# Squares on TensorE, sums on GpSimd, a gather from unscaled rows and a new order of issue in a fused convolution and selection kernel

## The chip, the cores and the metric

The kernel runs on one core of a Trainium2 chip. The metric is the time of one execution on the device in microseconds (us), the median of several; a profile of one execution goes with each kernel. A run counts as slow when it is over 1.5% above the fastest run of the same kernel.

The names of engines in the profile's lines are PE (TensorE's matrix products), PEld (its weight loads), DVE (VectorE), ACT (ScalarE), POOL (GpSimd) and SP (the engine that issues most DMAs). PSUM holds the tiles that TensorE's products are written to (`ps`, `pq`, `pg` in the lines), and an evacuation is the operation that copies or multiplies them out of it.

## The reference, cut to what matters

```python
h = layernorm(A_q) * (1 + ca) + sa                      # 2048 tokens x 640
x = A_q + ga * (h * (long_conv(short_conv(A_k) * A_v, ssm_k) + ...))   # two FFTs, product, inverse FFT
h = layernorm(x) * (1 + cb) + sb
r = h @ w_r;  idx = the 8 tokens with the largest r
y = (silu(h[idx] @ w_gate) * (h[idx] @ w_up)) @ w_down * sigmoid(r[idx])
out = x + gb * (h, with y added at the 8 rows)
```

So there is a long front that makes the convolution, block by block of 128 columns (five blocks), with Fourier products on TensorE; a middle in which the last sums x are formed and the second layernorm's sums and sums of squares are taken; and an end: root, choice of the eight rows, their gather and projections, the blend of all rows, and a scatter-add of eight rows into the output.

## The kernel before: the parts that matter

All steps are generators, and one string gives the order in which their pieces are issued. A star after a name means "on VectorE" for pieces that can go to either engine.

```python
# ORDER, its last lines (letters: BT inverse product, AT last products and sums, R row products,
# P complex product, S/SV/SA squares, BS/BL base, T choice to scatter, N normalised rows, F blend,
# LU load of U, WG/WD weights; new in the change: AA the adds of AT, GR a square step on TensorE)
#  ... BT4:2 P4:2 R0 AT2:2
#  BT4:2 LU3 AT3 R1 AT3 R1 R2* BS*:2 R2 R3* LU4 AT4:2 BS* S:3 R3 R4* SV R4 S SA:2 WD BS:3 T BS:2 BL N:5 N* T N*
#  WG N* N:2 T N N* N:3 N* F T F:3 BL F T:2 F:3 T:4

psum = tile_pool(bufs=4)                       # four double PSUM buffers for everything
T2 = ring.tile([P, 8, 2, P], BF, tag="T2")     # ONE buffer

def t_P(b):                                    # complex product, for each half of a block
    V.tensor_tensor(out=T2, in0=X, in1=Hi, op=mult)
    V.tensor_tensor(out=X,  in0=X, in1=Hr, op=mult)
    V.tensor_tensor(out=Xr, in0=Xr, in1=T2[:, :, 1, :], op=subtract)
    V.tensor_tensor(out=Xi, in0=Xi, in1=T2[:, :, 0, :], op=add)

def t_AT(b):                                   # [cut: 16 products into ps]
    V.tensor_tensor(out=t, in0=ps, in1=h[...], op=mult)
    V.tensor_tensor(out=xq[:, :, cc], in0=xq[:, :, cc], in1=t, op=add)

def squares(b0, nb, ms):                       # ScalarE; 9 rows of one block by VectorE statistics
    for m in ms:
        nc.scalar.activation(out=junk, in_=xq[:, m, ...], func=Square, accum_out=dst[:, m:m+1])

def t_T():                                     # [cut]
    rsqrt(rs2, vv)                             # seed and three Newton steps
    # [cut: r_bf, choice of 8, onehot]
    matmul(pxs[:, b, :], lhsT=xn(m)[:, b*P:(b+1)*P], rhs=onehot[:, m, :])   # gather of NORMALISED rows
```

Of the kernel before, what the change touches and what calls it, by code (L numbers as in the profile page):

```python
# [9 lines left out]
P = 128  # L10
# [25 lines left out]
LK0 START TC RA DIAG0 RA TAB0 RAT LG0 LK1 C0:2 TAB0 G0 LG1 TAB1:2 G0*:2 LX G0* DIAG1 C1:2 DIAG2 BG0 LXA0 BG0*  # L36
IT* Sx RAT G1 BG0 G1:3 DIAG3 Sx:2 IT*:2 X0 X0* BG1 LXA1 X0 X0* BG1 LX:2 LW BG1:2 LK2 Sx:4 X1 BX0 BX0*:2 BX0
P0:2 X1:3 BG0 LG2 LW LK3 C2:2 MOD Sx DIAG4 Sx LX LW Sx:2 P0:2 G2:3 BT0 BX1 LXA2 C3 G2 BX1 BT0 Sx:2 BT0 BX1 MOD
LW MOD LW P1 BX1 X2:3 Sx:4 LG3 C3 X2 BT0 MOD LW LXA3 P1:2 LK4 BG2:2 BX2 LG4 P1 BX2:3 BG2:2 MOD:2 OG BT1 P2:4
G3 X3:2 BT1 COL G3:2 H:3 G3 G4:2 C4 BT1 H BT1 H X3:2 C4 LXA4 LU0 G4:2 BG3 BX3:2 H:3 BT2 H:4 BX3 BG3:3 BT2:3 P3  # L40
AT0 P3 LU1 X4:4 AT0 BX3 BG4 P3:2 BX4:3 BG4 AT1 WG BT3 LU2 BT3:3 BG4:2 P4:2 AT1 BX4 R0 BT4:2 P4:2 R0 AT2:2
BT4:2 LU3 AT3 R1 AT3 R1 R2* BS*:2 R2 R3* LU4 AT4:2 BS* S:3 R3 R4* SV R4 S SA:2 WD BS:3 T BS:2 BL N:5 N* T N*
WG N* N:2 T N N* N:3 N* F T F:3 BL F T:2 F:3 T:4
# [17 lines left out]
def _kernel_body(ctx, tc, A_q, A_k, A_v, A_shift_k, A_ssm_k, A_ssm_D,  # L61
# [5 lines left out]

    def dump(name, ap):
        if name in DBG:
            nc.sync.dma_start(out=DBG[name], in_=ap)  # L70
# [6 lines left out]
    psum = ctx.enter_context(tc.tile_pool(name="psum", bufs=4, space=bass.MemoryType.PSUM))  # L77

    def ps_tile(shape, dtype=F32):
        return psum.tile(list(shape), dtype, name="ps", tag="ps")  # L80
# [69 lines left out]
    bcol = const.tile([NB * NSEL, 1], F32, name="bcol")  # L150
    gb40 = const.tile([NB * NSEL, P], BF, name="gb40")
# [41 lines left out]
    def t_TC():  # L193
# [9 lines left out]
        G.tensor_scalar(out=bcol[:], in0=bcol[:], scalar1=-MAGIC, scalar2=None, op0=ALU.add)  # L203
        G.tensor_scalar(out=cinfo[:, 0:1], in0=mC[:], scalar1=128.0, scalar2=None, op0=ALU.mult)
# [60 lines left out]
    As, HXs, Uds, uAs, diags = {}, {}, {}, {}, {}  # L265
# [21 lines left out]
    def t_C(b):  # L287
        kT, vT = kTs[b], vTs[b]
        kvT = ring.tile([P, S_TOK], BF, name="kvT", tag="V")
        for i2 in range(2):  # L290
            ps = ps_tile([P, 2, 512])
            for i in range(2):
                n0 = 16 + 512 * (2 * i2 + i)
                for j in range(4):
                    nc.tensor.matmul(ps[:, i, :], lhsT=diags[b][:, j, :], rhs=kT[:, n0 - j:n0 - j + 512],  # L295
                                     start=(j == 0), stop=(j == 3))
            V.tensor_tensor(out=kvT[:, 1024 * i2:1024 * i2 + 1024], in0=ps[:].rearrange("p a b -> p (a b)"),  # L297
                            in1=vT[:, 1024 * i2:1024 * i2 + 1024], op=ALU.mult)
# [24 lines left out]
    T2 = ring.tile([P, 8, 2, P], BF, name="T2", tag="T2")  # L323

    def t_P(b):
        hx = HXs[b]
        for hk in range(2):
            ks = slice(8 * hk, 8 * hk + 8)
            X = hx[:, ks, :, 1, :]
            Xr, Xi = hx[:, ks, 0, 1, :], hx[:, ks, 1, 1, :]  # L330
            Hr, Hi = (hx[:, ks, i:i + 1, 0, :].to_broadcast([P, 8, 2, P]) for i in range(2))
            V.tensor_tensor(out=T2[:], in0=X, in1=Hi, op=ALU.mult)
            V.tensor_tensor(out=X, in0=X, in1=Hr, op=ALU.mult)  # L333
            yield
            V.tensor_tensor(out=Xr, in0=Xr, in1=T2[:, :, 1, :], op=ALU.subtract)
            V.tensor_tensor(out=Xi, in0=Xi, in1=T2[:, :, 0, :], op=ALU.add)
            yield

    def t_BT(b):
        hx = HXs[b]  # L340
        Ud = Uds[b] = dram.tile([P, M, 256], BF, name="Ud%d" % b)
        for hk in range(2):
            U = ring.tile([P, 8, 256], BF, name="U", tag="K", bufs=5)
            for kk in range(2):
# [8 lines left out]
                if kk == 1:  # L353
                    nc.gpsimd.dma_start(out=Ud[:, 8 * hk:8 * hk + 8, :], in_=U[:])  # L354
# [15 lines left out]
    ssq = small.tile([P, 2, M], F32, name="ssq")  # L370
# [4 lines left out]
    def t_AT(b):  # L375
        h = h_["h"]
        c0 = b * P
        for hb in range(2):
            uA = uAs[b][hb]
            ps = ps_tile([P, 2, M, 32])  # L380
            for bb in range(8):
                o = ps[:, bb // 4, :, (bb % 4) * 8:(bb % 4) * 8 + 8]
                for cs in range(2):
# [3 lines left out]
            t = ring.tile([P, M, 64], BF, name="t", tag="K", bufs=5)  # L387
            cc = slice(c0 + hb * 64, c0 + hb * 64 + 64)
            V.tensor_tensor(out=t[:].rearrange("p m (g j) -> p m g j", g=2), in0=ps[:].rearrange("p g m j -> p m g j"),  # L389
                            in1=h[:, :, cc].rearrange("p m (g j) -> p m g j", g=2), op=ALU.mult)  # L390
            V.tensor_tensor(out=xq[:, :, cc], in0=xq[:, :, cc], in1=t[:], op=ALU.add)  # L391
            yield

    def junk():
        if "junk" not in h_:
            h_["junk"] = ring.tile([P, S_TOK], BF, name="junk", tag="V")
        return h_["junk"]

    def squares(b0, nb, ms):

        dst = ssq[:, 0 if b0 == 0 else 1, :]
        n = nb * P
        for m in ms:
            nc.scalar.activation(out=junk()[:, 0:n], in_=xq[:, m, b0 * P:b0 * P + n], func=ACT.Square,  # L404
                                 accum_out=dst[:, m:m + 1])

    def t_S():
        for q in range(4):
            squares(0, 4, range(4 * q, 4 * q + 4))
            yield  # L410

    def t_SV():
        st = small.tile([P, 9, 2, 3], F32, name="st4")
        sq = small.tile([P, 9, 2], F32, name="sq4")
        for i in range(9):
            V.bn_stats(out=st[:, i].rearrange("p e s -> p (e s)"), in_=xq[:, 7 + i, 512:640])
        V.tensor_tensor(out=sq[:], in0=st[:, :, :, 1], in1=st[:, :, :, 1], op=ALU.mult)
        V.scalar_tensor_tensor(out=sq[:], in0=sq[:], scalar=64.0, in1=st[:, :, :, 2], op0=ALU.mult, op1=ALU.add)
        V.tensor_tensor(out=ssq[:, 1, 7:16], in0=sq[:, :, 0], in1=sq[:, :, 1], op=ALU.add)
        yield  # L420

    def t_SA():
        for ms in (range(0, 3), range(3, 7)):
            squares(4, 1, ms)
            yield
# [25 lines left out]
    def t_R(b):  # L451
# [3 lines left out]
        xT = ring.tile([P, M, P], BF, name="xT", tag="K", bufs=5)  # L455
        evac(xT[:], pt[:])
        yield
        pr = ps_tile([P, M, 3])
        for m in range(M):
            nc.tensor.matmul(pr[:, m, :], lhsT=xT[:, m, :], rhs=wcol[:, b, :], start=True, stop=True)  # L460
# [40 lines left out]
    def t_COL():  # L501
# [22 lines left out]
        onesf = early[:, 9728:9984].bitcast(F32)  # L524
        nc.gpsimd.memset(onesf, 1.0)
        pr = ps_tile([P, 2, 512])
        nc.tensor.matmul(pr[:, 0, 0:2], lhsT=onesf, rhs=red[:], start=True, stop=True)
# [26 lines left out]
    def rsqrt(dst, vv, name):  # L554
# [5 lines left out]
        V.tensor_scalar(out=vv[:], in0=vv[:], scalar1=-0.5, scalar2=None, op0=ALU.mult)  # L560
        y = yi[:].bitcast(F32)
        a = small.tile([P, n], F32, name=name + "a")
        for it in range(3):
            V.tensor_tensor(out=a[:], in0=y, in1=y, op=ALU.mult)
            V.tensor_tensor(out=a[:], in0=a[:], in1=vv[:], op=ALU.mult)
            o = dst if it == 2 else y
            V.scalar_tensor_tensor(out=o, in0=a[:], scalar=1.5, in1=y, op0=ALU.add, op1=ALU.mult)
# [10 lines left out]
    def t_S1():  # L578
# [5 lines left out]
        rsqrt(rs1[:], var1, "n1")  # L584
# [3 lines left out]
    def t_H():  # L588
        h = h_["h"] = big.tile([P, M, D], BF, name="h", tag="h")
        for m4 in range(4):  # L590
# [7 lines left out]
            V.tensor_tensor(out=hq, in0=hq, in1=sg[:, None, :].to_broadcast([P, 4, D]), op=ALU.add)  # L598
# [20 lines left out]
    rs2, nm2 = tiny("rs2"), tiny("nm2")  # L619
# [17 lines left out]
    def t_F():  # L637

        for j in range(8):
            x2 = xq[:, 2 * j:2 * j + 2, :]  # L640
            V.tensor_tensor(out=x2, in0=xn(2 * j, 2).rearrange("p (m d) -> p m d", m=2),  # L641
                            in1=gbo[:, None, :].to_broadcast([P, 2, D]), op=ALU.mult)
            V.tensor_tensor(out=x2, in0=x2, in1=h_["base", j // 4][:, 2 * (j % 4):2 * (j % 4) + 2, :], op=ALU.add)  # L643
            if j % 2 == 1:
                nc.sync.dma_start(out=out_d[:, 2 * j - 2:2 * j + 2, :], in_=xq[:, 2 * j - 2:2 * j + 2, :])
# [207 lines left out]
```

## Time and profile before

| | us |
|---|---|
| time, median of 3 runs (lowest, highest) | 186.27 (185.97, 188.59) |
| span of the profiled run | 183.9 |
| last inverse product (BT4) leaves TensorE: the front | 131.40 |
| from there to the start of `tot`, the variance: the middle | 22.03 |
| from `tot` to the end of `r_bf`: the root | 3.16 |
| from there to the end of the last blend F: the end | 18.59 |
| from there to the end of the span: the finish | 8.72 |

The five rows add up to the span. One more row, from a table by stretches of time, is wanted for comparison (columns: stretch, its length, busy time and number of instructions of PE, PEld, DVE, ACT, POOL, then granted clock, share of the DMA engines, GB/s):

```profile
0.00:131.40 131.40, 113.84 (x1134) 90.64 (x1134) 116.77 (x188) 103.20 (x112) 28.50 (x72) 0.97 0.92 234
```

VectorE works 116.77 of the front's 131.40 us and idles for 14.6.

### The profile page before, as it was taken

Reading aid. Unit: us, or ns where it says so; the run is one execution under the profiler, and the core shown is the slowest. Engines: PE = TensorE matmul, PEld = TensorE weight load, DVE = VectorE, ACT = ScalarE, POOL = GpSimd, SP = SyncE. Lnnn points to the kernel's source line nnn. Section 1 sums busy time; section 2 is a strip of 40 time slices with the busy share of each in tenths; the row PEclk is TensorE's granted clock in tenths of the full one; section 3 lists DMA queues with packets and bytes.
Section 4 is the critical chain, followed back from the end, with each engine's and each line's share of the span. In section 5 each row is a group of like instructions: output and inputs, shape, how many; then the busy total and the mean of one; then the engine's idle time right before and its main releaser. Section 6 shows DMA issues by size and latency. Waiting matters only on the chain.

```text
span 183.9 us, 4109 instructions
## 1 busy us (share of the span) xinstructions
PE 144.0 (78%) x1664; PEld 112.5 (61%) x1664; DVE 157.7 (86%) x283; ACT 136.2 (74%) x180; POOL 33.2 (18%) x81
## 2 busy tenths in 40 slices
PE   0669989985989999939999969999679578165850
PEld 0225979952768679837679759998577342024840
DVE  5869998988979899977599999989979996999930
ACT  4368789792897979775599979999448999996000
POOL 7997500005001022010010020020200102100003
PEclk9999999999999999995799999999999999955555
DMA  6999989999999999992041999994768099705540
GB/s 108 152 204 278 313 186 326 272 198 274 265 292 320 338 304 309 176 200 114 0 171 61 212 320 324 368 338 183 200 261 224 8 293 362 310 4 219 207 153 2
DMA packets 68668, 40.68 MB, mean 221 GB/s; under 512 B 44904, under 2 KB 64808, under 8 KB 68648
## 3 DMA queue, kind: packets, MB, share of 16 engines
q1 hardware_dynamic: 65160, 35.15, 72.7%
q0 software_dynamic: 1520, 5.25, 7.7%
q10 hardware_dynamic: 1968, 0.01, 0.7%
q8 instruction: 13, 0.21, 0.5%
q14 instruction: 7, 0.06, 0.1%
HBM read 24.67 MB, written 10.50 MB: 191 GB/s over the span
## 4 chain that ended last, share of the span: by engine, by line
DVE 27%; DMA 27%; PE 24%; ACT 12%; issue 6%; SPq 2%; POOLq 1%; POOL 0%; DVEq 0%; ACTq 0%
DMA kT<-in_A_k_dram 9%; PE ps L295 8%; ACT junk L404 7%; DMA kvd<-kvT 7%; DMA uA<-Ud 6%; DVE kvT L297 4%; DVE st L581 4%; PE ps L274 3%; PE ps L314 3%; DVE xq L641 3%; DMA Ud<-U 3%; DVE xq L643 3%; PE ps L384 2%; ACT U L58 2%; ACT A L58 2%
## 5 line engine op out<-in xcount | busy, mean ns | idle before, releaser
L58 ACT CAST A<-ps 128x1024 bf16<-128x1024 f32 x35 | 33.6, 1030 | 8.5 <-PE ps L274 8.5
L58 ACT CAST HX<-ps 128x1024 bf16<-128x1024 f32 x37 | 35.9, 1054 | 2.8 <-PE ps L318 2.8
L314 PE MATMUL ps<-A,FT 128*128 128x256 bf16 x160 | 36.2, 272 | 0.4 <-DVE kvT L297 0.4
L318 PE MATMUL ps<-A,FT 128*128 128x128 bf16 x160 | 35.0, 219 | 0.0
L316 PE MATMUL ps<-A,FT 128*128 128x128 bf16 x160 | 35.0, 219 | 0.0
L295 PE MATMUL ps<-kT,dg 128*128 128x512 bf16 x80 | 21.6, 426 | 7.0 <-DMA kT<-in_A_k_dram 7.0
L58 ACT CAST U<-ps 128x1024 bf16<-128x1024 f32 x20 | 19.8, 1048 | 5.0 <-PE ps L350 2.3
L295 PEld LDWEIGHTS <-dg 128*128 128x128 bf16 x80 | 8.5, 108 | 17.4 <-issue 3.8
L354 POOL DMA_DIRECT2D Ud<-U x10 | 5.7, 572 | 72.9 <-ACT U L58 62.9
L348 PE MATMUL ps<-IT,HX 128*128 128x256 bf16 x80 | 18.1, 273 | 0.8 <-DVE kvT L297 0.8
L350 PE MATMUL ps<-IT,HX 128*128 128x256 bf16 x80 | 18.1, 273 | 0.0
L297 DVE TENSOR_TENSOR kvT<-ps,vT 128x1024 bf16<-128x1024 f32 x10 | 12.1, 1220 | 6.9 <-PE ps L295 5.7
L318 PEld LDWEIGHTS <-FT 128*128 128x128 bf16 x160 | 15.7, 98 | 1.8
L316 PEld LDWEIGHTS <-FT 128*128 128x128 bf16 x160 | 15.6, 98 | 0.9 <-issue 0.8
L314 PEld LDWEIGHTS <-FT 128*128 128x128 bf16 x160 | 15.7, 98 | 0.3
L237 POOL TENSOR_SCALAR dg<-ident,shk_f 128x128 bf16<-128x128 bf16 x16 | 10.3, 659 | 20.0 <-PE ps L295 20.0
L384 PE MATMUL ps<-RAT,uA 128*128 128x128 bf16 x160 | 10.4, 219 | 4.2 <-DMA uA<-Ud 4.2
L404 ACT ACTIVATE junk<-xq 128x512 bf16<-128x512 bf16 (+1 forms) x23 | 12.2, 533 | 2.0 <-DVE xq L391 1.3
L389 DVE TENSOR_TENSOR t<-ps,h 128x1024 bf16<-128x1024 f32 x10 | 12.2, 1218 | 1.7 <-PE ps L384 1.6
L581 DVE BATCH_NORM_STATS2 st<-xq 128x6 f32<-128x320 bf16 x32 | 13.2, 478 | 0.5 <-DMA xq<-in_A_q_dram 0.5
L274 PE MATMUL ps<-RA,gA 128*128 128x256 bf16 x80 | 12.3, 309 | 1.5 <-DVE gA L281 1.5
L333 DVE TENSOR_TENSOR HX<-HX 128x2048 bf16<-128x2048 bf16 x10 | 12.2, 1225 | 0.4
(218 smaller groups left out, 308.6 us busy)
## 6 DMA issues: line engine op xcount, KB each, us to landing
Ud<-U POOLq DMA_DIRECT2D x10, 512.0 KB, 6.0
uA<-Ud SPq DMA_DIRECT2D x10, 512.0 KB, 6.5
early<-in_w_mod_dram SPq DMA_DIRECT2D x6, 800.0 KB, 7.3
gA<-in_A_ssm_k_dram SPq DMA_DIRECT2D x5, 512.0 KB, 5.0
kvd<-kvT SPq DMA_DIRECT2D x10, 256.0 KB, 3.9
xq<-in_A_q_dram SPq DMA_DIRECT2D x4, 640.0 KB, 6.4
xA<-kvd SPq DMA_DIRECT2D x5, 512.0 KB, 4.8
out_dram<-xq SPq DMA_DIRECT2D x4, 640.0 KB, 3.1
```

The lines of the kernel that those rows point to most:

```text
L58: self.nc.scalar.copy(out=out, in_=in_)
L274: nc.tensor.matmul(ps[:, bb // 2, :, (bb % 2) * 8:(bb % 2) * 8 + 8], lhsT=src[:, 4 * g4 + bb, :], rhs=RA[:].rearrange("p k c e -> p (k c) ...
L295: nc.tensor.matmul(ps[:, i, :], lhsT=diags[b][:, j, :], rhs=kT[:, n0 - j:n0 - j + 512], start=(j == 0), stop=(j == 3))
L297: V.tensor_tensor(out=kvT[:, 1024 * i2:1024 * i2 + 1024], in0=ps[:].rearrange("p a b -> p (a b)"), in1=vT[:, 1024 * i2:1024 * i2 + 1024], ...
L314: nc.tensor.matmul(ps[:, i], lhsT=FT[:, 0, k2, :], rhs=A[:, 2 * k2:2 * k2 + 2, u, :], start=True, stop=False)
L316: nc.tensor.matmul(ps[:, i, 0, :], lhsT=FT[:, 1, k2, :], rhs=A[:, 2 * k2 + 1, u, :], start=False, stop=False)
L318: nc.tensor.matmul(ps[:, i, 1, :], lhsT=FT[:, 2, k2, :], rhs=A[:, 2 * k2, u, :], start=False, stop=True)
L348: nc.tensor.matmul(ps[:, i, :], lhsT=hx[:, k2, 0, 1, :], rhs=IT[:, k2, 1:3, :].rearrange("p a b -> p (a b)"), start=True, stop=False)
L350: nc.tensor.matmul(ps[:, i, :], lhsT=hx[:, k2, 1, 1, :], rhs=IT[:, k2, 0:2, :].rearrange("p a b -> p (a b)"), start=False, stop=True)
L384: nc.tensor.matmul(o, lhsT=uA[:, bb, cs * P:(cs + 1) * P], rhs=RAT[:, cs, :].rearrange("p (m e) -> p m e", e=8), start=(cs == 0), stop=(cs ...
L404: nc.scalar.activation(out=junk()[:, 0:n], in_=xq[:, m, b0 * P:b0 * P + n], func=ACT.Square, accum_out=dst[:, m:m + 1])
L581: V.bn_stats(out=st1[:, m, hf, :], in_=xq[:, m, hf * 320:hf * 320 + 320])
```

## The change

The intent: take the squares from ScalarE (TensorE forms small products of the transposed rows, whose diagonals are the sums of squares), take sums from VectorE (starred ones go to GpSimd), make the gather independent of the normalised rows, shorten the root, and reorder everything.

```diff
-LK0 START TC RA DIAG0 RA TAB0 ...                  (the whole order is new)
+LK0 START RA LG0 DIAG0 ... LG3 TC P1* ...          (TC, small constants on GpSimd, comes late)
+... BT4* BT4 AT1 AA1* AT1 R0* LU3 AA1 AT2*:2 AA2* LU4
+R0 R1 WG AT3 GR AA2 R1 AT3 AA3* R2 AT4 GR AT4 AA3* AA4* R2 R3* BS AA4 GR R3 R4* GR BS GR WD GR R4 BS:4 T:2 N*
+BS:2 N*:2 T BL F N:5 BL N:3 T N F T:2 N:4 F:6 T:4
+def off(): return nc.gpsimd if evac.vector else V
+def times(out, acc, other):          # starred: ScalarE copies acc first, VectorE multiplies; else as before
-psum bufs=4
+psum: three double buffers "ps", one single bank "pq" for small products, one single bank "pg"
-V.tensor_tensor(out=Xr, ...); V.tensor_tensor(out=Xi, ...)          (t_P; the adds of t_AT and t_H alike)
+off().tensor_tensor(out=Xr, ...); off().tensor_tensor(out=Xi, ...)
-nc.gpsimd.dma_start(out=Ud...)
+(nc.sync if b == NB - 1 else nc.gpsimd).dma_start(out=Ud...)
-squares(...) on ScalarE, bn_stats on VectorE
+def t_GR():                          # one step for each block, 64 products; squares' sums stay in PSUM
+    for m in range(16):
+        for j in range(4):
+            matmul(pg[32j:32j+32, m, :], lhsT=xT[:, m, 32j:32j+32], rhs=xT[:, m, 32j:32j+32], tile_position=(0, 32j))
+    after the last: V multiply by a diagonal mask, V reduce -> ssq
-rsqrt: three Newton steps
+rsqrt: two steps of higher order, constant folded into the users
-matmul(pxs, lhsT=xn(m) ...)                         gather of normalised rows
+matmul(pxs, lhsT=xq[:, m, ...] ...)                 gather of unscaled rows; their scales and shifts are
+sel = onehot * (rs2, nm2); reduce; matmul(ones, sel2); five small ops give xsT
-store of four row groups after every second F    ->  +store of two after every F
```

## The prediction

> **What bounds the kernel now.** I read the page first (busy shares, slices), then a table by stretches of time, then the chain that ended last, then each engine's timeline from 128 us on.
>
> ```profile
> span 183.9 us, 4109 instructions
> PE 144.0 (78%) x1664; PEld 112.5 (61%) x1664; DVE 157.7 (86%) x283; ACT 136.2 (74%) x180; POOL 33.2 (18%) x81
> ...
> 100.00:120.00 20.00, 18.02 (x224) 16.45 (x222) 19.69 (x23) 18.20 (x20) 1.43 (x3) 1.00 0.98 290
> ...
> 140.00:150.00 10.00, 6.53 (x119) 5.33 (x117) 9.93 (x15) 9.59 (x27) 0.63 (x1) 1.00 0.55 149
> 150.00:160.00 10.00, 5.93 (x29) 2.36 (x26) 7.97 (x42) 9.78 (x24) 1.51 (x5) 1.00 1.02 375
> 160.00:170.00 10.00, 5.29 (x86) 3.44 (x86) 9.69 (x19) 8.66 (x11) 0.52 (x2) 0.55 0.27 98
> ```
>
> The columns of the table are PE, PEld, DVE, ACT, POOL busy, then granted clock, DMA share, GB/s. VectorE (DVE) is the fullest engine in the front and again after 160 us; GpSimd (POOL) is nearly empty; TensorE's clock falls to 0.55 at the end.
>
> Three stages follow. Front, to about 131.4 us, where the last inverse-transform products (BT4) leave TensorE: from the windows, VectorE is busy 115.4 of the first 130 us. Middle, to 153.4, where the variance can start. End, the root, the choice of 8 rows, the normalised rows N, the blend F and the last scatter. The ends of the last two:
>
> ```profile
> 143.42 1.07 PE L384 MATMUL ps<-RAT,uA 128*128 128x128 bf16 x16 [0.71 <-DMA uA<-Ud]
> ...
> 138.33 0.63 ACT L404 ACTIVATE junk<-xq 128x512 bf16<-128x512 bf16 x1 [1.31 <-DVE xq L391]
> ...
> 153.43 0.17 DVE L653 SCALAR_TENSOR_TENSOR tot<-ssq 128x16 f32<-128x16 f32 x1 [1.09 <-ACT junk L404]
> ...
> 167.82 0.22 PE L715 MATMUL ps<-onehot,IT 128*128 128x8 bf16 x2 [0.62 <-ACT IT L633]
> ...
> 174.36 0.82 DVE L643 TENSOR_TENSOR xq<-xq,base 128x1280 bf16<-128x1280 bf16 x1
> 175.10 0.26 DVE L740 TENSOR_TENSOR hT<-gs,ps 128x112 bf16<-128x112 bf16 x1
> ```
>
> The last block of sums waits for a DMA round trip (U written, uA read): U ready 132.6, second half used at 143.4. The squares fill ScalarE for 15 us, 138.3 to 153.3, and VectorE's variance waits 1.09 us for them: their removal alone is worth about that, because the row products for the last block reach VectorE only at 151.7. The gather waits repeatedly for rows normalised by ScalarE. But the last blend op ends at 175.2 and hT comes right after it, while the second projection was done at 174.4: gather and blend are nearly tied, so speeding the gather alone gains under 1 us.
>
> **What the Trainium skill says.** (1) "SBUF — State Buffer", Who interferes with whom: VectorE and GpSimd share a port pair under an exclusive lock; a VectorE op with two SBUF inputs shuts out a GpSimd op that reads SBUF, and the reverse. The trace agrees: a 16-column GpSimd add, usually 0.27 us, took 1.24 us, ending just after the VectorE product that began before it:
>
> ```profile
> 68.57 1.22 DVE L333 TENSOR_TENSOR HX<-HX 128x2048 bf16<-128x2048 bf16 x1
> ...
> 68.68 1.24 POOL L281 TENSOR_TENSOR gA<-gA,Dt 128x16 bf16<-128x16 bf16 x1 [2.16 <-DMA gA<-in_A_ssm_k_dram]
> ```
>
> (2) "GPSIMD Engine Reference", Elementwise — side-by-side cycle accounting: about 2.6 cycles an element for two inputs at 1.2 GHz. My estimate for 1024 columns is 1024 x 2.6 / 1.2 = 2.2 us, against 0.69 on VectorE here; no large GpSimd add is in this trace. (3) "TensorE: Matmul & The Clock Gate", Wait — 56ns, not 53.3ns?: starts of small matmuls are never closer than about 25 ns. Here 70 projection products take 2.0 us, 28.6 ns each, agreeing roughly. (4) "TensorEngine Tiling (Array Packing)", Restrictions: column tiling disables fast weight load. No product here is tiled, so its cost is open.
>
> **The change part by part.** I counted the schedule's steps with start-to-start times from the timelines: a PSUM evacuation 1.13 us on VectorE, 0.91 on ScalarE; a complex-product half 2.4 (two products) plus 1.22 (two sums); a block half of AT 1.13 plus 0.61 for the add.
>
> Front. Evacuations put on VectorE before the end of BT4 rise from 11 (3 G, 1 BG, 3 IT, 2 X, 2 BX) to 20 (6 G, 1 BG, 3 IT, 6 X, 3 BX, 1 BT): +10.2 us. Six pairs of sums of the complex product go to GpSimd: -7.3. AT steps before the end of BT4 fall from six to two, and one add is done by then: 10.4 down to 2.9, so -7.5. Small differences (one convolution evacuated by ScalarE, two shorter roots) take about 1. Summed over the two orders, the large work is 112.8 us before BT4 ends now and 107.0 after: -5.8. The front now loses 131.4 - 112.8 = 18.6 us to idling and small ops; with the same loss BT4 would end at 125.6. The better order can trim it, lock and PSUM can add.
>
> Middle. AT and its add for four blocks are moved here, and the squares. Each new square step is 64 products of 32x32 (four column tiles for each of 16 row groups); at 28 ns, 1.8 us, five of them 9 us. From the end of BT4, TensorE has eight AT steps of 0.9 (7.2), five transposes of 0.9 (4.5), five row products of 0.44 (2.2), 9.0 for squares and two base steps of 0.87 (1.7): 24.6 us. Then multiply and reduce over 512 columns, about 0.65 each[...], and the last row sum 0.2: 1.5. The variance can start at +26.1, against 153.4 - 131.4 = 22.0 now. TensorE, not ScalarE, would set this stage: +4.1. ScalarE's 15 us are freed, but were only just on the path.
>
> Root. In before the chain from tot to r_bf is 15 small ops, 153.43 to 156.59 = 3.2 us. The new one is tot, vv, the seed, seven root ops, two more: 12 at 0.21 = 2.5. Gain 0.7.
>
> End, from r_bf to the last blend, now 156.6 to 175.2 = 18.6 us with VectorE full. New: rs2 and nm2 hide behind the transpose (0.45 idle), choice 1.56, three N 1.2, ranks 1.6, F0 1.65, onehot 0.4, F1 1.65, the selection by scales 2 x 0.42, wait for its product 0.6, three small ops 0.6, gather's rest 0.4, two small ops and a copy 0.35, six F at 1.63 = 9.8: 21.1. That is +2.5: two fewer N on VectorE do not pay for the new small ops and their waits. The gather no longer waits for N, so the projections end about 5 us before VectorE gets to hT, but hT is still issued after the last F, so this slack is unused. From F7 to the end 8.7 us now; with the last store half as large, perhaps 8.4: -0.3. Single-bank buffers serialise pg, silu and pu (about 0.5 us), inside the slack.
>
> Sum with an unchanged share of losses: -5.8 + 4.1 - 0.7 + 2.5 - 0.3 = -0.2 us: a tie.
>
> **Rivals.** A: that tie; against it stands what the sum leaves out. The new order spreads the loads and convolutions: before, the second convolution waited for kT from 28.2 to 39.4 us on the chain, and the first 21 us held about 9 us of idling and small ops. The final blocks of AT, delayed on purpose, fill the 10 us round trip of the last block, and U4 is stored by the sync queue instead of GpSimd. If idling in the front falls from about 14 to 8, BT4 ends near 120; this order looks searched for and I believe more in it than in unchanged losses: 178 to 181 us in all. B: the lock. Eighteen GpSimd ops (12 of P, 6 adds), about 40 us in all, relieve VectorE of 11 us; where a VectorE op with two SBUF inputs follows at once, it stands for up to 2.2 us. Ten such collisions of 1 us cost 10: 188 or more. What speaks against it is that many of these GpSimd ops are followed on VectorE by evacuations or statistics, which do not need the second input. C: only three double PSUM buffers instead of four make TensorE wait for late evacuations; ScalarE's smaller load (about 130 to 114 us) speaks against more than 2 us. D: tiled products slower than the issue floor because weights load slowly (60 ns a pair): 3.8 us a step, +10 us in the middle, about 190. If instead they pair well and TensorE keeps its full clock, the middle is as long as now and the time 177.
>
> **Range and chances.** I take A's searched order as the likeliest, about -6 us for the front beyond the tie, give back a little for lock and PSUM, and predict 180.5 us (186.27 now, -3.1%). The tie lies at 186, B and D above it. Range 173.5 to 187. Chances: faster by over 2% (below 182.5) 0.64, within 2% 0.27, slower 0.09.
>
> **What would show it.** Last BT product near 120 to 126 us; VectorE in the front over 90% busy; no ScalarE squares; square steps near 1.8 us each; variance start some 24 to 26 us after BT4, with TensorE the releaser; r_bf 2.5 us after it; last blend 21 us after r_bf, with short VectorE waits for the scales' product; hT directly after the last blend although the projections were long done. GpSimd adds well above 2.2 us, or VectorE products above 1.22, would show the lock. The prediction is wrong if BT4 ends after 128, if square steps pass 3 us, or if the end from r_bf takes no longer than now.

## The result

| | before | changed |
|---|---|---|
| median of 4 runs (lowest, highest), us | 186.12 (184.87, 188.59) | 203.68 (203.35, 204.6) |
| ratio of the fast runs | | 1.098, 95% interval 1.091 to 1.105 |

A ratio is the mean time of one kernel's fast runs over that of the other's fast runs of the same rounds, so not quite the ratio of the medians. The changed kernel is 9.8% slower; the prediction had said 3.1% faster, and its range ended at 187. Both profiled runs were fast ones:

| stage | before | changed | difference | predicted |
|---|---|---|---|---|
| front, to the last BT product | 131.40 | 138.96 | +7.56 | -5.8, and about -6 more |
| middle, to `tot` | 22.03 | 30.13 | +8.10 | +4.1 |
| root, to `r_bf` | 3.16 | 2.59 | -0.57 | -0.7 |
| end, to the last F | 18.59 | 22.14 | +3.55 | +2.5 |
| finish | 8.72 | 8.08 | -0.64 | -0.3 |
| span | 183.9 | 201.9 | +18.0 | |

The head of the changed kernel's page (busy time, share of the span and number of instructions of each engine):

```profile
span 201.9 us, 4734 instructions
PE 153.4 (76%) x1986; PEld 117.8 (58%) x1986; DVE 156.5 (77%) x259; ACT 123.1 (61%) x133; POOL 73.8 (37%) x101
```

And its stretches of time, the front first, in the columns explained above:

```profile
0.00:138.96 138.96, 113.38 (x1040) 87.38 (x1041) 115.42 (x174) 95.82 (x103) 56.41 (x87) 0.94 0.86 222
...
140.00:150.00 10.00, 8.11 (x204) 7.59 (x204) 9.38 (x10) 3.85 (x4) 6.64 (x5) 1.00 1.00 265
150.00:160.00 10.00, 7.54 (x160) 5.85 (x161) 5.36 (x6) 1.87 (x1) 6.25 (x4) 0.85 0.69 240
160.00:170.00 10.00, 6.97 (x251) 4.64 (x251) 4.03 (x12) 2.36 (x3) 0.79 (x4) 0.84 0.60 208
```

Work did leave VectorE and ScalarE (the latter from 136.2 to 123.1 us), and nearly the same 157 us of VectorE now stretch over a longer span. In the front VectorE's busy time is only 1.35 us less than before (115.42 against 116.77), and its idle time has grown from 14.6 to 23.5 us: -1.35 + 8.9 is the front's +7.56. (VectorE is busy for 83% of this front.) In the middle, from 150 us on, no engine is full any more; there somebody must be waiting for something that is no engine's work.

**Front.** The timeline of the changed kernel (columns: start, duration, engine, line, operation, output and inputs; in brackets the idle time before and what ended it):

```profile
49.97 4.67 POOL L261 TENSOR_SCALAR dg<-ident,shk_f 128x128 bf16<-128x128 bf16 x8
54.61 0.62 POOL L215 TENSOR_SCALAR DM<-arow,pidx 128x128 f32<-128x128 f32 x1
...
61.43 2.12 POOL L360 TENSOR_TENSOR HX<-HX,T 128x1024 bf16<-128x1024 bf16 x1
63.51 2.12 POOL L361 TENSOR_TENSOR HX<-HX,T 128x1024 bf16<-128x1024 bf16 x1
65.67 1.23 DVE L357 TENSOR_TENSOR T<-HX 128x2048 bf16<-128x2048 bf16 x1 [7.26 <-POOL HX L361]
```

Read it from the last line upwards. VectorE wants to write the product buffer T (`T2` in the code) for the next half, and there is only one; the sums that read it, L360 and L361, stand on GpSimd at 2.12 us each. GpSimd is late because it first builds diagonals (4.67 us) and then the small constants of TC, 54.61 to 61.43. VectorE idles 7.26 us. Over the kernel the ten T products wait 8.0 us (7.7 of it for GpSimd), where they waited 0.2 before. A second place shows the lock between the two engines (the Trainium skill, "SBUF — State Buffer", Who interferes with whom):

```profile
87.43 2.23 POOL L360 TENSOR_TENSOR HX<-HX,T 128x1024 bf16<-128x1024 bf16 x1 [13.22 <-DVE HX L358]
87.60 2.41 DVE L509 TENSOR_TENSOR modv<-modv 128x640 bf16<-128x640 bf16 x1
89.63 2.36 POOL L361 TENSOR_TENSOR HX<-HX,T 128x1024 bf16<-128x1024 bf16 x1
90.12 2.21 DVE L521 TENSOR_TENSOR modv<-modv 128x640 bf16<-128x640 bf16 x1
...
93.74 0.56 PE L536 MATMUL ps<-red,onesf 128*128 128x2 f32 x2 [5.56 <-DVE junk L533]
```

Two VectorE products of 640 columns take 2.41 and 2.21 us instead of 0.48 while GpSimd's sums run; each ends 0.35 us after the sum that ran beside it. This is 3.66 us of the work that the page counts as busy. TensorE waits behind them. The same two kinds of products in VectorE's timeline of the kernel before, neither with a wait in front:

```profile
71.04 0.48 DVE L497 TENSOR_TENSOR modv<-modv 128x640 bf16<-128x640 bf16 x1
...
125.51 1.23 DVE L332 TENSOR_TENSOR T<-HX 128x2048 bf16<-128x2048 bf16 x1
```

**Middle.** TensorE's timeline of the changed kernel, its products only:

```profile
149.24 0.26 PE L471 MATMUL pq<-wcol,xT 128*128 128x3 bf16 x5 [1.04 <-issue]
149.36 1.05 PE L409 MATMUL ps<-RAT,uA 128*128 128x128 bf16 x16
150.25 1.06 PE L465 MATMUL ps<-ident,xq 128*128 128x128 bf16 x16
151.15 1.06 PE L409 MATMUL ps<-RAT,uA 128*128 128x128 bf16 x16
152.13 0.66 PE L430 MATMUL pg<-xT 128*32 128x32 bf16 x64
152.73 0.79 PE L409 MATMUL ps<-RAT,uA 128*128 128x128 bf16 x11
155.98 0.45 PE L409 MATMUL ps<-RAT,uA 128*128 128x128 bf16 x5 [2.46 <-issue]
...
167.10 0.28 PE L430 MATMUL pg<-xT 128*32 128x32 bf16 x14 [3.03 <-issue]
```

Two things. A square step, 64 small products, takes 0.60 us from its start to the next start (152.13 to 152.73), 9.4 ns a product; I had predicted 1.8. And TensorE stops three times, 6.53 us together, in the midst of a group of equal products, and the profile shows nothing that it waits for ("issue"). Count the products between the first two stops: 5 + 16 + 16 + 16 + 64 + 11 = 128. Each product has a weight load, so that is 256 instructions. Between the second and the third stop the same count gives 255 products, twice that. The DMA view lists packets of a queue called "instruction"; for the stretch 153.55 to 153.60 us, just after the second stop began at 153.52, it has this line (queue, kind: packets, MB, share):

```profile
q8 instruction: 1, 0.02, 135.8%
```

Searching the middle in steps of 0.05 us finds such a packet at 146.50, 153.55, 157.05 and 164.50; TensorE's three restarts follow the first, the second and the fourth by 2.7, 2.4 and 2.6 us (after the third, nothing stopped). In the whole execution there are 15 such packets, and 13 in the kernel before, where TensorE has 3328 products and loads, 13 times 256. So the stops look like TensorE's own supply of instructions. The Trainium skill, page "Runtime: NRT & Kernel Launch", section "Instruction fetch mechanics", says that each engine's instructions come in blocks of 16 KiB, 256 instructions, by a DMA queue of its own, and that the price of crossing a block is "mostly hidden" because issuing is slower than filling. The size of the block agrees with this trace. "Mostly hidden" agrees for most crossings (in the kernel before no such stop exceeds 0.3 us), but not for these three: TensorE used up the 128 products after its first restart in 4.3 us.

The rest of the middle: TensorE is busy 22.69 us in it, stops 6.53, waits 0.78 for a DMA: 30.0 of 30.13. In the kernel before it was busy for 15.90 us of this stage, so the new order also brings 6.8 us more of TensorE's work into it.

**End.** VectorE's timeline of the changed kernel after `r_bf` (171.68):

```profile
172.95 0.28 DVE L687 CAST T<-pq 16x128 f32<-16x128 bf16 x1 [0.98 <-PE pq L685]
...
180.94 0.61 DVE L736 TENSOR_REDUCE sel<-T 128x16 f32<-128x256 f32 x1
183.33 0.20 DVE L749 TENSOR_TENSOR xa<-pq,mc 128x40 f32<-128x40 f32 x1 [1.78 <-PE pq L740]
...
193.00 0.82 DVE L659 TENSOR_TENSOR IT<-IT,base 128x1280 bf16<-128x1280 bf16 x1
193.75 0.26 DVE L772 TENSOR_TENSOR hT<-gs,pq 128x112 bf16<-128x112 bf16 x1
```

VectorE waits 0.98 us for the transposed `r` and 1.78 for the product of the scales, and hT follows the last blend directly, as predicted.

### The profile page after: what moved, and what is told of

The parts are those of the page before. It is cut to its first block, busy times and chain, and to the rows that moved or that the text cites. A ratio compares the mean times of both kernels' runs of the same rounds, so it can differ in the third digit from the quotient of the medians.

```text
span 201.9 us, 4734 instructions
## 1 busy us (share of the span) xinstructions
PE 153.4 (76%) x1986; PEld 117.8 (58%) x1986; DVE 156.5 (77%) x259; ACT 123.1 (61%) x133; POOL 73.8 (37%) x101
## 4 chain that ended last, share of the span: by engine, by line
DVE 36%; PE 30%; DMA 12%; POOL 11%; issue 8%; POOLq 1%; ACT 1%; SPq 0%; DVEq 0%; ACTq 0%
PE ps L319 5%; DVE T L357 5%; DVE HX L358 4%; PE ps L338 4%; DMA xA<-kvd 4%; POOL HX L361 3%; DVE kvT L79 3%; DMA uA<-Ud 3%; DMA kT<-in_A_k_dram 3%; DVE h L613 2%; POOL dg L261 2%; POOL HX L360 2%; PE ps L409 2%; PE ps L342 2%; PE ps L340 2%
## 5 line engine op out<-in xcount | busy, mean ns | idle before, releaser
L338 PE MATMUL ps<-A,FT 128*128 128x256 bf16 x160 | 37.6, 279 | 6.7 <-DVE A L57 6.4
L342 PE MATMUL ps<-A,FT 128*128 128x128 bf16 x160 | 35.7, 223 | 0.0
L340 PE MATMUL ps<-A,FT 128*128 128x128 bf16 x160 | 35.7, 223 | 0.0
L59 ACT CAST A<-ps 128x1024 bf16<-128x1024 f32 x28 | 27.8, 1016 | 12.4 <-issue 6.6
L360 POOL TENSOR_TENSOR HX<-HX,T 128x1024 bf16<-128x1024 bf16 x6 | 13.9, 2321 | 24.6 <-DVE HX L358 24.6
L59 ACT CAST U<-ps 128x1024 bf16<-128x1024 f32 x19 | 18.6, 1040 | 3.1 <-PE ps L375 2.9
L373 PE MATMUL ps<-IT,HX 128*128 128x256 bf16 x80 | 18.9, 280 | 0.3 <-DVE HX L360 0.2
L375 PE MATMUL ps<-IT,HX 128*128 128x256 bf16 x80 | 18.8, 280 | 0.3 <-DVE HX L361 0.3
L59 ACT CAST base<-ps 128x1024 bf16<-128x1024 f32 x10 | 9.8, 1013 | 14.9 <-PE ps L446 14.8
L357 DVE TENSOR_TENSOR T<-HX 128x2048 bf16<-128x2048 bf16 x10 | 12.2, 1220 | 8.0 <-POOL HX L361 7.7
L57 DVE CAST A<-ps 128x1024 bf16<-128x1024 f32 x12 | 14.6, 1221 | 3.1 <-PE ps L298 3.0
L420 POOL TENSOR_TENSOR xq<-xq,t 128x1024 bf16<-128x1024 bf16 x6 | 13.0, 2180 | 6.8 <-DVE t L79 5.2
```

The lines of the kernel that those rows point to most:

```text
L57: self.nc.vector.tensor_copy(out=out, in_=in_)
L59: self.nc.scalar.copy(out=out, in_=in_)
L338: nc.tensor.matmul(ps[:, i], lhsT=FT[:, 0, k2, :], rhs=A[:, 2 * k2:2 * k2 + 2, u, :], start=True, stop=False)
L340: nc.tensor.matmul(ps[:, i, 0, :], lhsT=FT[:, 1, k2, :], rhs=A[:, 2 * k2 + 1, u, :], start=False, stop=False)
L342: nc.tensor.matmul(ps[:, i, 1, :], lhsT=FT[:, 2, k2, :], rhs=A[:, 2 * k2, u, :], start=False, stop=True)
L357: V.tensor_tensor(out=T2[:], in0=X, in1=Hi, op=ALU.mult)
```

## The experiments

Fourteen kernels. All gave the right result. "BT" is the end of the front in each profile; ratios are to the kernel before in the same rounds, whose median lay between 185.1 and 187.1 us.

How far these figures carry: the 95% intervals of the ratios reach 0.5 to 2.4% to either side, and the record's own verdict is "slower" for the changed kernel and d2, "same" for d1 and "unclear" for all others. A ratio counts fast runs alone. In the rounds of a1, a2, a4 and b3 this leaves 3 of the other kernel's 7 runs, in those of a6, a7, b6 and c1 4 of 11; by the medians of all runs these ratios are 1.1 to 2.1 points lower (a1 1.066, a7 1.059, b6 1.004). The rounds ran on different chips. The stages come from one profile for each kernel: c1's front, whose code differs from that of the kernel before by a shorter root alone, is 1.7 us shorter, so I read nothing from smaller differences of fronts.

| kernel | us | ratio | BT | middle | root | end | finish |
|---|---|---|---|---|---|---|---|
| before | 186.12 | | 131.40 | 22.03 | 3.16 | 18.59 | 8.72 |
| changed | 203.68 | 1.098 | 138.96 | 30.13 | 2.59 | 22.14 | 8.08 |
| a1 nothing on GpSimd | 199.39 | 1.080 | 133.90 | 31.96 | 2.60 | 22.17 | 8.07 |
| a2 constants early | 200.65 | 1.094 | 135.46 | 29.86 | 2.59 | 22.07 | 7.92 |
| a7 both (slow profile) | 197.48 | 1.070 | 133.48 | 32.23 | 2.60 | 22.27 | 8.02 |
| b1 before, three PSUM buffers | 188.46 | 1.013 | 134.10 | 20.60 | 3.15 | 18.86 | 10.19 |
| a3 squares on ScalarE | 204.9 | 1.102 | 136.86 | 29.72 | 2.60 | 23.71 | 8.11 |
| a4 weights loaded late | 202.38 | 1.097 | 137.91 | 29.65 | 2.77 | 22.14 | 8.13 |
| a6 squares doubled | 209.32 | 1.137 | 137.75 | 36.18 | 2.59 | 21.21 | 8.27 |
| a5 gather of normalised rows | 202.89 | 1.092 | 137.13 | 29.86 | 2.60 | 21.57 | 8.44 |
| b3 old order, all new parts | 201.03 | 1.092 | 133.77 | 28.90 | 2.64 | 23.48 | 8.61 |
| b4 b3, store on GpSimd | 191.95 | 1.029 | 134.11 | 21.65 | 2.64 | 23.63 | 8.77 |
| b6 b4, gather of normalised rows | 187.38 | 1.015 | 133.66 | 21.05 | 2.66 | 19.08 | 7.95 |
| c1 before, short root, small stores | 186.35 | 1.012 | 129.70 | 21.42 | 2.61 | 19.44 | 8.83 |
| d1 b6, four buffers (slow profile) | 185.36 | 0.998 | 132.48 | 22.58 | 2.65 | 21.68 | 8.11 |
| d2 a7, four buffers (slow profile) | 198.43 | 1.069 | 134.51 | 32.21 | 2.60 | 22.39 | 7.89 |

The theory after reading the traces: the front loses to GpSimd (its sums hold the single T buffer, and its lock stretches VectorE's work), the middle to TensorE's supply of instructions, the end to the small operations of the new gather. The rivals: the three PSUM buffers in the front; in the middle the squares as such, or the 4 MB of weights whose transfers lie in the way of the fetches; in the end the order.

### Front: a1, a2, b1, a7

a1 sends all sums and adds back to VectorE; a2 only moves the constants; b1 takes one PSUM buffer from the kernel before.

```diff
 a1
-    return nc.gpsimd if evac.vector else V
+    return V
 a2
-LK0 START RA ...  LG3 TC P1*
+LK0 START TC RA ...  LG3 P1*
 b1 (on the kernel before)
-psum bufs=4
+psum bufs=3
```

> The changed kernel with all eighteen GpSimd sums (12 of the complex product, 6 block adds) given back to VectorE, order kept. Theory 1 (GpSimd halves cost the front: VectorE's next product waits for GpSimd's sums, 7.26 us at 58 us, and VectorE products of COL ran 2.4 and 2.2 us instead of 0.5 while GpSimd summed): the last BT product moves from 139.0 to 134 or earlier although VectorE gets 11 us of work back; time 196 to 199 us. Rival (the order and the three PSUM buffers make the front long whatever GpSimd does): the last BT product stays at 138 to 144, time 203 to 208 us.

> The changed kernel with the GpSimd constants (TC, 6.8 us at 54.6 to 61.4) moved back right behind START, nothing else. Theory 1 (the queue in front of the sums counts): VectorE's wait at 58 us falls from 7.3 to about 4.3, the last BT product comes 3 us earlier, time about 200.5 us. Rival: the 3 us are absorbed by a later wait (the convolution that follows, COL), time 203 to 204 us.

> The kernel before with three double PSUM buffers instead of four, nothing else. Theory 4 (the missing fourth buffer costs the front, since all parts in the old order had the last BT product 2.4 us late): last BT product at 133 to 135, time 188 to 190 us. Rival (that delay came from the other parts): within 1 us of before, 185.5 to 187.

a1 shortens the front by 5.06 us, a2 by 3.5. In a1 the stretched products are back at 0.48 us and T waits 0.5 us in all: VectorE has 2.4 us more to do in the front and idles 7.4 us less. (a1's profile is of the longest of its four runs, a2's of the shortest. The middle of a1 is 1.8 us longer than the changed kernel's, so its time falls by less than its front.) b1 lengthens the front of the kernel before by 2.7 us and its time by 1.3%. Since a1 and a2 could be one loss seen from two sides (a late GpSimd costs only where something is on GpSimd), a7 does both.

> The changed kernel with both of the front's suspects undone: no vector half of work on GpSimd, and the small constants of GpSimd built at the start as before. Alone they took 5.1 and 3.5 us from the front. If they are two separate losses, the last inverse product ends at 130 to 131 us, like in the kernel before, and what remains of the front's loss is nothing; the time is 195 to 197. If both were one and the same queue on GpSimd, seen from two sides, it ends at 133 to 134 as with the first alone, and the time is 198 to 200; then the other 2.5 us are the three buffers, which alone cost the kernel before 2.7.

The front ends at 133.48, where a1's ended at 133.90, which speaks for one loss; but this profile fell on the longest of a7's five runs, some 2 us above the others. The medians speak for two: 6.2 us below the changed kernel, where a1 alone has 4.3 and a2 3.0; but these are medians of different chips, and a2's ratio (1.094, 1.071 to 1.118) is not apart from the changed kernel's. The time of 197.48 lies between the two cases. So a1's part is shown, by its trace and its time; how much of a2's comes on top of it is not settled.

### Middle: a3, a4, a6

```diff
 a3: the squares of the kernel before in the new order
-... GR ... GR ... GR ... GR ... GR ... GR
+... S:4 ... SV SA:2 ...
 a4: weights after the squares
-R0 R1 WG AT3 ... BS GR WD GR R4 BS:4 T:2
+R0 R1 AT3 ... BS GR GR R4 BS:4 T WG WD T
 a6: each product twice
-for j in range(4):
+for j in list(range(4)) * 2:         # and the sums halved afterwards
```

> The changed kernel with the squares back on ScalarE (and a few of the last block on VectorE, as before), the 320 small products gone. Theory 2 in its new form (late weights did not cure TensorE's stops, so it runs short of instructions because these small products use up 256 instructions, 128 products with their weight loads, in under 4 us): the three stops of 1.0, 2.5 and 3.0 us vanish. The time need not fall: the last sums of block 3 are ready 15 us after the last BT product, and 15 us of squares on ScalarE follow, so the variance starts 28 to 31 us after BT and the time is 200 to 204 us. Rival (the stops belong to this order of AT steps and transposes, not to the squares): stops of 1 to 3 us stay.

> The changed kernel with the loads of the second projection's and of the last projection's weights (4 MB) issued behind the root instead of in the middle. Theory 2 (TensorE's three unexplained stops of 1.0, 2.5 and 3.0 us at 148, 153 and 164 us, which lie 128 and 255 products apart, are waits for its instructions, whose transfers stand behind the 4 MB): the stops shrink to under 1 us in sum, the variance starts about 24 us after the last BT product instead of 30.1, time 197 to 199 us if the late weights arrive in time, which they should (needed some 15 us later). Rival (TensorE takes its instructions faster than they can be fetched at all): the stops stay at 1 to 3 us each, time 203 us or more.

> The changed kernel with every square product issued twice (320 more products; the sum of squares is halved again afterwards, so the result stays right). A product took 9.4 ns, so the added work is 3.0 us. Theory, TensorE runs out of instructions: 320 products with their weight loads are 640 instructions, two and a half blocks of 256 more in the middle, and each block that is used up within a few us costs a stop of 1 to 3 us: five or six stops instead of three, the middle 36 to 40 us instead of 30.1 and the time 209 to 214. Rival, the stops come from something that is there once whatever the number of products (a semaphore, a DMA): still three stops of 6.5 us in all, the middle 33, the time 206 to 207.

a3: no stop of TensorE is left, but the middle is no shorter. VectorE's timeline tells why:

```profile
160.10 0.20 DVE L493 TENSOR_TENSOR rsum<-rsum,pq 128x48 f32<-128x48 f32 x1
...
166.58 0.17 DVE L688 SCALAR_TENSOR_TENSOR tot<-ssq 128x16 f32<-128x16 f32 x1 [6.07 <-ACT junk L433]
```

The last row sum is ready at 160.10, 23.2 us after BT, where the changed kernel needs 29.8. Removed were 3.0 us of squares on TensorE and 6.5 of stops, and a3's order also issues the two base steps (2.8 us) behind the row sums; in return TensorE waited 5.1 us in this stretch for copies and loads, where it had waited 0.8. What comes out is 6.6 us, so a3 is no clean measure of what the stops alone cost. But ScalarE can start the squares only at 151.4, as the new order forms the sums late, and takes until 166.5. So the stage is bound twice in this order: by TensorE's supply, or by ScalarE.

a4: the middle is 29.65 us and the stops are 1.31, 0.40 and 3.90. They move, but hardly shrink. That the weights' transfers are in the way of the fetches has fallen as the main cause.

a6: five stops in place of three, as the theory said and the rival did not. TensorE's timeline of this kernel:

```profile
147.33 0.56 PE L433 MATMUL pg<-xT 128*32 128x32 bf16 x53 [0.51 <-issue]
...
153.85 1.10 PE L433 MATMUL pg<-xT 128*32 128x32 bf16 x117 [2.59 <-issue]
...
157.31 0.45 PE L409 MATMUL ps<-RAT,uA 128*128 128x128 bf16 x5 [1.63 <-issue]
...
167.93 0.78 PE L433 MATMUL pg<-xT 128*32 128x32 bf16 x74 [4.05 <-issue]
...
171.39 0.80 PE L433 MATMUL pg<-xT 128*32 128x32 bf16 x77 [0.34 <-issue]
```

The stops sum to 9.1 us. The counts between them are again 128, 128, 255 and 128 products, and the instruction packets at 144.80, 151.50, 154.90, 165.35 and 169.05 us lie 2.3 to 2.6 us ahead of the five restarts. The middle is 36.18 us, 6.05 longer, of which the added products are about 3 and the added stops 2.6. (A sixth packet, at 158.30, has no stop after it.) The stops go with the number of instructions, fall on the block's boundary, and each ends shortly after a block's packet: I take their cause as shown. What is not shown is why the packet comes so late; at the two long stops of the changed kernel it was seen only after TensorE ran dry (153.55 after 153.52, 164.50 after 164.07), at the short one 1.7 us before (146.50, dry at 148.20).

### The order: b3, b4, b6

b3 has all new parts of the code in the old order of issue (each AT followed by its add on VectorE, a square step after each block's transpose). b4 also lets GpSimd store the last U again. b6 takes the gather of the normalised rows back.

```diff
 b3
-ORDER = the new one
+ORDER = the old one, "AT2 AA2 AT2 AA2 ...", "R0 GR AT2", "R1 GR R2*", "R2 GR R3*", "R3 GR R4* GR R4 GR"
 b4
-(nc.sync if b == NB - 1 else nc.gpsimd).dma_start(out=Ud...)
+nc.gpsimd.dma_start(out=Ud...)
 b6
-matmul(pxs[:, b, :], lhsT=xq[:, m, ...], ...); sel ...; five small ops
+matmul(pxs[:, b, :], lhsT=xn(m)[:, ...], ...); two small ops
-F in place, stored from the normalised rows
+F into xq, stored from there
```

> All parts of the change (squares on TensorE, gather from the sums, short root, single banks, three double buffers) in the old order of issue, without GpSimd sums and without ScalarE in front of the products. Theory 3 (the new order is what costs): 183 to 187 us, the last BT product within 2 us of 131.4. Rival (the parts cost: buffers in the front, instruction stops in the middle): 190 us or more.

> All parts of the change in the old order of issue, but the last block's U stored by GpSimd's queue as before (in the earlier run on the sync queue it stood in front of the loads of block 3 and TensorE waited 7.1 us for them). If that queue was the cause of that run's middle of 28.9 us: middle 21 to 23 us, no 7 us wait, end 23.5 us as there, time 192 to 194 us. Rival (the squares lengthen the middle in any order): middle 26 us or more, time 197 or more.

> The run with the old order of issue and the store on GpSimd (191.95 us), but the gather takes the normalised rows again, as before. If the 5 us by which its end was longer than the kernel before's (23.63 against 18.59) are the gather from the sums, the end is 18.5 to 19.5 and the time 187 to 188. If they came from the single banks or from somewhere else in the end, it stays at 22 to 23.5 and the time at 190.5 to 192.

b3 is slow for a reason of its own making: the last U's store stood on the SP queue ahead of another block's load, and TensorE waited 7.11 us for that load (at 140.87). So the move of this store belongs to the new order and is harmful in the old one. b4 removes it and is the telling run: the same squares on TensorE, the same single banks, and not one stop, with a middle of 21.65 us, 0.4 shorter than the kernel before. (TensorE's work in this stage is 16.18 us there, not 22.69, as more of the AT products come before the end of BT4.) Its square steps stand apart, between products that wait anyway; the last one in TensorE's timeline:

```profile
152.96 0.68 PE L422 MATMUL pg<-xT 128*32 128x32 bf16 x64 [1.39 <-DVE xT L49]
```

So squares on TensorE are sound; what the new order does is to pack them, the delayed AT products and the transposes so densely that three blocks of instructions are used up faster than they come.

b6 then shows the price of the gather from unscaled rows in the old order: its end is 19.08 us, b4's 23.63. In b4 the selection by scales stands behind five blends on VectorE (two in the changed kernel), and TensorE waited 6.07 us for it. On VectorE the selection takes 1.0 us and the wait for its product 1.77; 1.26 of the 4.55 us are a longer wait for the transposed `r` (1.63 against 0.37), which need not be the gather's. What is left in b6 against the kernel before is the front, 2.3 us, the size of b1's effect.

### End: a5

```diff
-gather, F and tail of ORDER of the changed kernel
+gather and F as in b6; "R4 BS:4 T BS:2 BL N:5 N* T N* N* N:2 T N N* N:3 N* F T F:3 BL F T:2 F:3 T:4"
```

> The changed kernel with the gather taken again from the normalised rows and the old order of issue from the root on (five rows normalised by VectorE, as before). Theory 5 (the new small VectorE operations and the wait for the scales' product lengthen the end, which the blend on VectorE bounds): from r_bf to the last blend 18.5 to 19.5 us instead of 22.1, time 199.5 to 201 us. Rival (the end is long because of its order or the single banks): 21.5 us or more, time 203 us.

The end is 21.57 us and not 18.5 to 19.5: a miss at first sight. The timeline (TensorE's and VectorE's lines) shows that I had built in a wait:

```profile
172.66 0.38 PE L458 MATMUL ps<-xq,ident 128*128 128x512 bf16 x1
172.97 0.22 PE L686 MATMUL pq<-ident,r_bf 128*16 128x128 bf16 x1
...
173.23 0.28 DVE L688 CAST T<-pq 16x128 f32<-16x128 bf16 x1 [2.87 <-PE pq L686]
```

`r_bf` was ready at 169.59, but its transpose stands behind base products in TensorE's queue, so VectorE waited 2.87 us where b6 waits 0.37 at the same place. Without those 2.5 us the end would be 19.07, b6's value. So I read a5 as agreeing with b6, but that is an argument from one wait; no run has this order with the transpose moved.

### A version that beats both: c1, d1; and the order alone: d2

```diff
 c1 (on the kernel before)
+root in two steps; store after every F; last F split, hT between its two operations
 d1 (on b6), d2 (on a7)
-three double buffers, single banks pq and pg
+four double buffers; from the first square step on the fourth holds pg; small products use a double buffer
```

> The kernel before with the parts that the study found good: the root in two steps with its constant folded in (0.57 us shorter there), one store for each pair of rows so that the last one is half as large (it landed 2.2 us after its issue instead of 3.6), and the product of the two projections placed between the two operations of the last blend. If these gains add, 0.6 from the root and 0.7 to 1.2 from the finish: 184.3 to 185.0 where the kernel before has 186.1. If the scatter waits for something else than the last store, only the root's part shows: 185.5.

> The changed kernel with nothing on GpSimd that was on VectorE, the constants built early, and four double PSUM buffers up to the first square step (the fourth then holds the sums of squares; small products take a double buffer as before). If the front's loss was these three parts and the new order itself neither gains nor loses, the last inverse product ends at 131 to 132 (131.40 in the kernel before), and the time is 195 to 196. If the new order really trims the idling as the prediction believed, it ends at 128 or earlier, and the time is 192 or less. If the order itself costs, it stays at 133.5 as with three buffers, and the time at 197 to 198. The middle keeps its stops in all three cases, 29 to 32 us.

> Squares on TensorE, two-step root, one store for each pair of rows, all in the old order of issue, with rows gathered as before and four double PSUM buffers up to the first square step. With three buffers this was 187.38 us, front 133.66. If the 2.3 us that its front loses are the buffers, the last inverse product ends at 131 to 131.6, the middle is 21 to 21.5, root 2.6, end 19 to 19.5, finish 8 to 8.5, and the time is 184.5 to 185.5, a little under the kernel before (186.1 to 186.6). If they are not, the front stays at 133 to 134 and the time at 187.

c1: the medians are the same (186.35 and 186.56). The ratio of 1.012 rests on a cut that calls 7 of the other kernel's 11 runs slow and 2 of 6 of this one, so I take it as no verdict; a gain it is not. The root is 0.55 us shorter, as in the changed kernel, and the end 0.85 longer. ScalarE's timeline of c1 has the reason:

```profile
151.00 5.56 ACT L58 CAST base<-ps 128x1024 bf16<-128x1024 f32 x6
...
156.41 4.19 ACT L639 ACTIVATE FT<-xq,nm,rs 128x640 bf16<-128x640 bf16 x5
```

The normalised rows cannot start before six base copies are done, whatever the root does; the chain of waits of this run goes through these two groups. And the halved last store took 3.40 us to land, hardly less than the 3.58 before: the finish is as long.

d1: 185.36 us, ratio 0.998 (0.993 to 1.004), as expected in time and no faster than the kernel before. Against b6 (1.015) the fourth buffer is worth about 1.7%, near the 2 to 3 us of b1; but b6's ratio rests on the same cut as c1's, and by the medians of all runs it is 0.3%. For the buffers speak the fronts of the four profiles with three of them in the old order, 133.66 to 134.11; their worth in time is not settled. d1's profile is of a slow run, so I read no stages from it.

d2: 198.43 us, ratio 1.069 (1.064 to 1.075), against a7's 1.070. The fourth buffer gives nothing here. With no sums on GpSimd, early constants and four buffers, the new order (with the new gather) is still nearly 7% slower than the kernel before. Of the three cases, the third came nearest: the time was to be 197 to 198 if the order itself costs. Its profile, too, is of a slow run (BT at 134.51), so the front's share of this is not known. The stops are not all that the new order costs in the middle: in a1's fast profile they sum to 5.5 us, 1.0 less than in the changed kernel, and its middle is 1.8 us longer, as TensorE waits 2.9 us for VectorE's adds, for a copy and for a DMA. (d2's slow profile points the same way: stops of 3.1 us, a middle of 32.21.)

## Why the prediction was wrong

**The front: the step that failed.** The prediction summed VectorE's work to 5.8 us less and then wrote, "The better order can trim it", and in rival A "this order looks searched for and I believe more in it than in unchanged losses". That term, the losses, was taken as 18.6 us or less; its change has the wrong sign. (The prediction's own signs said so too: BT4 was to end by 128 and VectorE to be over 90% busy in the front; it was 138.96 and 83%.) By its own count (107.0 us of large work), the losses were 138.96 - 107.0 = 32.0. Measured directly, VectorE's work fell by 1.35 us, not 5.8, because two products took 3.66 us longer under the lock and lesser things did the rest, and its idling rose by 8.9. The counts were right: 20 evacuations, and eighteen GpSimd operations of 39.9 us in all against "about 40" (2.12 us for one alone, where the prediction's estimate was 2.2). What was not asked is who waits for them. The argument against rival B, that GpSimd's sums are often followed on VectorE by operations that need no second input, was about the lock alone; the larger loss is a plain one of data, 7.7 us of waits for a buffer of which there is one, written again by the very engine that was to be relieved. a1, which takes both losses away, wins 5.06 us; the traces tell them apart.

Rival C, the buffers, said not more than 2 us; in the old order it is 2.7 in b1's front (1.3% of the time), and b6's front agrees. In the new order d2 finds nothing. The front's +7.56 can be written as a1's 5.06 and 2.5 for the buffers, but since d2 does not win those 2.5 back, that split is not shown; what the new order itself does to the front stays open, as the profiles of a7 and d2 fell on slow runs.

**The middle: right direction, two terms mis-sized.** TensorE does set the stage. The term "9.0 for squares" is 3.0 us from start to start (five steps of about 0.60), since the floor of 25 to 28 ns a product that I applied does not hold for these products in four column tiles: they start every 9.4 ns. In its place stand 6.5 us of stops that no term of the sum had (a6, and their absence in a3 and b4). AT, transposes and row products came about as counted (0.9, 0.9 and 0.45 us from start to start). The two base steps before the last squares took 2.8 us instead of 1.7, as one ran at a granted clock of 0.50, where a product took 0.43 us from start to start and not 0.22. (A third ran beside VectorE's multiply and reduce and held up nothing.) From the end of BT4 to the last square TensorE was busy 21.0 us, stopped 6.53 and waited 0.78, where the prediction had a sum of 24.6 and no stop; the multiply, reduce and last row sum after it took 1.7 us against 1.5.

**Root.** -0.57 against -0.7: right, in this kernel. c1 shows that it is worth nothing where ScalarE's base copies set the start of the normalised rows.

**End and finish.** +3.55 against +2.5: the mechanism was right, the waits were too small. The scales' product cost 1.78 us of waiting instead of 0.6, and the transpose 0.98 instead of 0.45. The finish was -0.64 against -0.3, but the reason given, the last store half as large, is not shown: c1 has that store and a finish of 8.83 us. hT stood directly behind the last blend, as said.

**Where the 9.8% are.** Undoing GpSimd's sums and the late constants leaves 7.0% (a7). In the old order, the gather from unscaled rows and three buffers leave 2.9% (b4), three buffers alone 1.5% (b6; 0.4% by medians), and without either nothing is left (d1). d2, which has the new order and the new gather but neither the sums on GpSimd nor the three buffers, stands at 6.9% where d1 stands at none. Of these 6.9%, the gather is 1.4% in the old order by the ratios of b4 and b6 and 2.4% by their times; in the new one a5 has 0.6%, which is within its interval. The rest, some 4.5 to 6%, is the new order, to which the last U's store on the SP queue belongs. Most of it lies in the middle (31.96 us in a1's fast profile, 22.03 before): sums delayed into it, and instructions packed there too densely. How these two share it is not shown.

## What to carry to other kernels

Before moving work to a slow, idle engine, ask which buffer it holds and whether the engine that is relieved must wait for exactly that buffer; a count of busy time cannot show it. Many tiny products are cheap on TensorE only while their instructions arrive: spread them between waits, and look for stops at multiples of 256 instructions when "issue" ends an idle time. And test an order apart from the parts that come with it: here the squares, the short root and the small stores in the old order tie with the kernel before, while the new order costs some 4.5 to 6% by itself.

## What the Trainium skill lacked or had wrong

- "Runtime: NRT & Kernel Launch", Instruction fetch mechanics: the crossing of a block is said to be mostly hidden, and no cost is given for one that is not. Here three crossings cost TensorE 1.0, 2.5 and 3.0 us, and with doubled squares five cost 9.1 us; it restarted 2.3 to 2.7 us after the block's packet was seen. That 256 instructions make a block agrees.
- "TensorE: Matmul & The Clock Gate", Wait — 56ns, not 53.3ns?: the floor of about 25 ns between starts is given there without an exception for products in column tiles: 64 of them in four column tiles took 0.60 us, 9.4 ns each. The page's part on packing does let products in different tiles run at once; the prediction applied the floor to them all the same.
- "TensorEngine Tiling (Array Packing)", Restrictions: that column tiling disables fast weight load is stated without its cost; here the 9.4 ns for each product contain its weight load.
